# Attention with a routed MoE on one core: the small blocks' first product in two column halves, and a new layout of the PSUM banks in the block loop

## The chip, the cores and the metric

One Trainium2 chip, one of its cores. The metric is the device time of one execution in microseconds (us). Before the change it is 514.08 us, the median of 3 runs (513.99 to 514.44).

## What is computed

Sigmoid attention over 8 batches and 12 heads of 448 tokens with 64 columns, whose result, 3584 tokens of 768 columns, goes through a mixture of experts with a skip:

```python
scores = scale * np.matmul(q, k.transpose(0, 1, 3, 2)) - np.log(S)
attn = 1.0 / (1.0 + np.exp(-scores))
x = np.matmul(attn, v)                  # then 3584 tokens x 768
do_compute = x @ w_skip > 0             # the other tokens are passed on
e_idx = np.argmax(xc @ w_gate, axis=1)  # xc: the tokens to compute; 8 experts
for e in range(8):
    h = np.maximum(xc[mask] @ w1[e], 0.0)         # 768 -> 1024
    y[mask] = gate_w[mask, None] * (h @ w2[e])    # 1024 -> 768
out[do_compute] = xc + y
```

## The kernel before

Up to about 290 us the kernel does the attention and, as each batch is ready, the routing logits. Two blocks of 128 tokens (b0, b1) of the first expert follow with a fixed program, and beside them the lists of tokens for each expert are made. From 313.64 us a loop (L1553 to L1555) runs blocks of tokens; each iteration reads a code word and takes one of four arms:

- FULL and SPLIT (function `block`, L1351): 128 rows. The weights have been split into two parts (wh, wl), the rows too (xh, xl), and each product is the sum of three. SPLIT converts the next expert's weights besides.
- HALF (`half`, L1468): at most 64 rows. The raw f32 weights are used; an f32 matmul leaves two records in the trace. Two matmuls at a time go to two groups of 64 columns of the array.
- FEW (`few`, L1408): at most 32 rows, likewise with raw weights, four matmuls at a time on four groups of 32 columns.

With this input there are fourteen: SPLIT, HALF, FULL, HALF, FULL, FEW, FULL, FEW, FULL, FEW, SPLIT, FEW, FULL, FEW. So seven are large, two HALF, five FEW.

A small block does, in this order on TensorE: the first product (rows times w1) into ph; six transposes of the next block's rows (turn_x, L492, from xn into pxt); the transposes of hs (into pht, a line in each of `few` and `half`: L1442, L1497); the second product (ht times w2) into py. ScalarE (ACT) does the relu from ph to hs (L1433, L1489) and, after the transposes, copies the turned rows to ht (L1444, L1503). Then it turns pxt into the next block's xh, with VectorE (DVE) making xl. SyncE (SP) issues the loads of the next weights: raw1 (`load_w1`, L1234) behind the first product, raw2 (`load_w2`) behind the second. GpSimd (POOL) fetches the rows and the record of coming blocks (`fetch`, from L1286 on) and scatters the results (`put`, `scatter`, L574). In the large blocks, DVE multiplies py by the gate into ys (`weigh_sum`, L1349), in two halves of 384 columns.

The order of the instructions of an arm is as written; semaphore waits between engines are added by the framework, from which instruction touches which tile. PSUM has eight banks of 512 f32 a partition. Here they are given to two two-bank tiles (`new_s`, [P, 2, 512], by turns s0 and s1), three single ones (`new_t`) and one single one (ps_b). In the loop, ph is two single tiles, py is one two-bank tile, pht is another (its second half and the free ph tile serve a small block's two turned parts as `turned = (pht[0], ph[1])`), and pxt is one tile of ps_b and one of new_t.

`addr_align` (L1159), ahead of part of b1's second product, places the code that follows at an offset in a fetch block of TensorE's instructions.

Of the kernel before, what the change touches and what calls it, by code (L numbers as in the profile page):

```python
# [10 lines left out]
F32 = mybir.dt.float32  # L11
# [3 lines left out]
AF = mybir.ActivationFunctionType  # L15
ALU = mybir.AluOpType
# [7 lines left out]
def kernel(  # L24
# [117 lines left out]
    def new_s(name):  # L142

        turn[0] ^= 1
        return ps_s.tile([P, 2, 512], F32, tag=f"s{turn[0]}", name=name)
# [102 lines left out]
    def new_t(name):  # L248

        if ps_t is None:  # L250
            return new_s(name)[:, 0, :]
        return ps_t.tile([P, 512], F32, tag="t", name=name)
# [236 lines left out]
    def turn_x(x, h, px):  # L489
        for j in range(3):  # L490
            i = 3 * h + j
            nc.tensor.transpose(  # L492
                px[:, j * P : (j + 1) * P], x[:, i * P : (i + 1) * P], ident
            )
# [43 lines left out]
    def gemm2(j, hh, hl, py):  # L538
        h, m = divmod(j, 4)
        js = slice(m * P, (m + 1) * P)  # L540
        kinds = ((hh, wh2), (hh, wl2), (hl, wh2))
        terms = [(n, o) for n in range(3) for o in range(2)]
        if j == NK2 - 1:
            terms.sort(key=lambda t: t[::-1])
        for n, o in terms:
            a, w = kinds[n]
            last = nc.tensor.matmul(  # L547
                py[:, o, :H2],
                a[h][:, js],
                w[j][:, o * H2 : (o + 1) * H2],  # L550
                start=(j == 0 and n == 0),
                stop=(j == NK2 - 1 and n == 2),
            )
        return last

    def finish(ys, py, gate, x):
        for o in range(2):
            s = slice(o * H2, (o + 1) * H2)
            nc.vector.scalar_tensor_tensor(
                ys[:, s], py[:, o, :H2], gate, x[:, s], op0=ALU.mult, op1=ALU.add  # L560
            )

    def gather(dst, idx, rows=NT):
# [248 lines left out]
    def new_ph(j):  # L812
        one = new_s(f"b{j}_ph")
        return [one[:, 0, :], ps_b.tile([P, 512], F32, tag="b", name=f"b{j}_ph1")]

    def relu0(h, ph):
        nc.scalar.activation(hs0[h], ph[h], AF.Relu)

# [33 lines left out]
    lg = turn_logits(lb, pl)  # L852
    store_rows(lb, NPAIR - 1, turn_rows(lb, NPAIR - 1))
    ph = new_ph(0)
    py = new_s("b0_py")
    gemm1(0, range(9), xh0, xl0, ph)
    rec, _ = rt = route(lb, lg)
    weigh_route(lb, rt)
# [292 lines left out]
    relu0(1, ph)  # L1151
    nc.vector.tensor_copy(rid[:, 1:2], recs[:, 1, 1:2])
    gather(xn, rid[:, 1:2])
    py = new_s("b1_py")
    for j in range(2):
        gemm2(j, hh0, hl0, py)
    turn0(1)
    nc.tensor.addr_align(bass.FETCH_BLOCK_INSTRUCTIONS, offset=0, max_nops=0)
    for j in range(2, NK2 - 3):  # L1159
        gemm2(j, hh0, hl0, py)  # L1160
    pxt = [ps_b.tile([P, 512], F32, tag="b", name="pxt0"), new_t("pxt1")]
    for h in range(2):
        turn_x(xc, h, pxt[h])
        hi_x(h, pxt[h], xh)
    for h in range(2):
        whole_x(h, [slice(j, j + 1) for j in range(3)])
# [55 lines left out]
    raw1 = [[raw1g[h, i // 3][:, i % 3, :] for h in range(2)] for i in range(NK1)]  # L1222
    raw2 = [raw2g[j // 2][:, j % 2, :] for j in range(NK2)]

    ph = [new_t(f"ph{h}") for h in range(2)]
    py = new_s("py")
    pht2 = new_s("pht")
    pht = [pht2[:, h, :] for h in range(2)]

    def next_expert(word):  # L1230
        return word & (NE - 1), (word & (2 * NE)) >> (2 * NE).bit_length() - 1
# [119 lines left out]
    def block(i, last):  # L1351


        def split1(js, h):
            if last:
                for j in js:
                    hi1(j, h)
                for j in js:
                    lo1(j, h)

        gemm1(0, range(G1), xh, xl, ph, last)
        relu(0, hs, ph)
        split1(range(3), 0)
        gemm1(1, range(9), xh, xl, ph, last)
        turn_h(0, hs, pht[0])
        split_h(0, pht[0], hh, hl)
        take_rec()
        split1(range(3, NK1), 0)
        gemm1(1, range(9, G1), xh, xl, ph, last)
        relu(1, hs, ph)  # L1370
        for h in range(2):
            turn_x(xn, h, pxt[h])
        fetch()
        split1(range(3), 1)
        gemm2(0, hh, hl, py)
        turn_h(1, hs, pht[1])
        split_h(1, pht[1], hh, hl)
        split1(range(3, NK1), 1)
        if last:
            for h in range(2):  # L1380
                whole_x(h, (slice(0, 3),))
            shift(dve)
        else:
            ready_x()
        for j in range(1, NK2):
            gemm2(j, hh, hl, py)
        if last:
            for j in range(2):
                hi2(j)
            for h in range(2):  # L1390
                hi_x(h, pxt[h], xh)
            for j in range(2, NK2):
                hi2(j)
            for j in range(4):
                lo2(j)
            for h in range(2):
                lo_x(h, pxt[h], xh, xl)
        else:
            shift(dve)
        for o in range(2):  # L1400
            weigh_sum(ys[:, o * H2 : (o + 1) * H2], py[:, o, :H2], recs[:, 0, 0:1])
        put(P)
        advance(1 if last else 2)
        if last:
            for j in range(4, NK2):
                lo2(j)

    def few(i, word):  # L1408

        nx = next_expert(word)  # L1410
        for o in range(2):
            nc.vector.tensor_copy(gate2[o * SM : (o + 1) * SM], recs[:SM, 0, 0:1])  # L1412
        take_rec()

        def quarter(dst, g, n, a, w, j, most):
            nc.tensor.matmul(  # L1416
                dst[g * SM : (g + 1) * SM, :n],
                a,
                w,
                start=(j == 0),  # L1420
                stop=(j == most - 1),
                tile_position=(0, g * SM),
            )

        Q1 = FF // 4
        for j in range(NK1):
            for g in range(4):
                s = slice((g % 2) * Q1, (g % 2 + 1) * Q1)
                quarter(ph[0], g, Q1, xf[:, j, :SM], raw1[j][g // 2][:, s], j, NK1)
        turned = (pht[0], ph[1])  # L1430
        parts = [slice(c * P, (c + 1) * P) for c in range(2)]
        for s in parts:
            nc.scalar.activation(hs[:, s], ph[0][:, s], AF.Relu)  # L1433
        for h in range(2):
            for g in range(2):
                load_w1(g, h, nx)
        for h in range(2):
            turn_x(xn, h, pxt[h])
        fetch()
        ht4 = ht[:, : 8 * SM].rearrange("p (c g t) -> p c g t", c=2, g=4)  # L1440
        for s, p in zip(parts, turned):
            nc.tensor.transpose(p[:, :P], hs[:, s], ident)  # L1442
        for s, p in zip(parts, turned):
            nc.scalar.activation(ht[:, s], p[:, :P], AF.Copy)  # L1444
        ready_x()
        shift(dve)

        for n, j in enumerate((0, 2, 1, 3)):
            for g in range(4):
                h, o = g // 2, g % 2  # L1450
                m = j + h * (NK2 // 2)
                quarter(
                    py[:, 0, :],
                    g,
                    H2,
                    ht4[:, j % 2, 2 * h + j // 2, :],
                    raw2[m][:, o * H2 : (o + 1) * H2],
                    n,
                    NK2 // 2,
                )  # L1460
        for g in range(4):
            load_w2(g, nx)
        nc.scalar.activation(yh, py[MD:, 0, :H2], AF.Copy, scale=gate2)
        nc.vector.scalar_tensor_tensor(yt, py[:MD, 0, :H2], gate2, yh, op0=ALU.mult, op1=ALU.add)
        put(SM)
        advance()

    def half(i, word):  # L1468
# [11 lines left out]
                tile_position=(0, g * MD),  # L1480
            )

        for j in range(NK1):
            for h in range(2):
                side(ph[0], h, H1, xf[:, j, :], raw1[j][h], j, NK1)
        turned = (pht[0], ph[1])
        parts = [slice(0, 2 * P), slice(2 * P, 4 * P)]
        for s in (slice(0, P), slice(P, 2 * P), parts[1]):
            nc.scalar.activation(hs[:, s], ph[0][:, s], AF.Relu)  # L1489
        for h in range(2):  # L1490
            for g in range(2):
                load_w1(g, h, nx)
        for h in range(2):
            turn_x(xn, h, pxt[h])
        fetch()
        for c in range(4):
            nc.tensor.transpose(  # L1497
                turned[c // 2][:, (c % 2) * P : (c % 2 + 1) * P],
                hs[:, c * P : (c + 1) * P],
                ident,  # L1500
            )
        for s, p in zip(parts, turned):
            nc.scalar.activation(ht[:, s], p[:, : 2 * P], AF.Copy)  # L1503
        ready_x()
# [3 lines left out]
        for n in range(NK2):  # L1508
            c, h = divmod(n, 2)
            m = h * (NK2 // 2) + c  # L1510
            for o in range(2):
                side(
                    py[:, 0, :],
                    o,
                    H2,
                    ht8[:, c, h, :],
                    raw2[m][:, o * H2 : (o + 1) * H2],
                    n,
                    NK2,
                )  # L1520
        for g in range(4):
            load_w2(g, nx)
        for o in range(2):
            s = slice(o * H2, (o + 1) * H2)
            weigh_sum(ys[:MD, s], py[o * MD : (o + 1) * MD, 0, :H2], recs[:MD, 0, 0:1])
        put(MD)
        advance()

# [55 lines left out]
```

## Time and profile before

| | |
|---|---|
| profiled execution, device time | 514.12 us |
| its span on the core | 512.4 us |
| median of the runs | 514.08 us |
| mean granted TensorE clock | 0.993 |
| TensorE (PE) busy | 499.9 us (98%) |
| DVE / ACT / POOL busy | 294.5 / 271.8 / 258.8 us |
| first of the loop's blocks starts | 313.64 us |
| last matmul of the loop's last block ends | about 503 us |

The timeline view gives, for each run of like instructions on an engine, the start in us from the span's start, the time until the last of them ends, the line, the operation, the output and input tiles, shapes and the count; in brackets the idle time ahead of it and what ended it. Matmuls overlap in the array, so that the time of a run is longer by a part of its last matmul than the distance to the next run.

### The profile page before, as it was taken

What the parts mean: (1) busy time and instruction counts of PE and PEld (TensorE: products, weight loads), DVE (VectorE), ACT (ScalarE), POOL (GpSimd) and SP (SyncE); (2) the same over time, 40 slices, a digit from 0 to 9 for tenths busy, and PEclk for the clock granted to TensorE, in tenths of its full rate; (3) what the DMA queues carried; (4) which work ended last, traced back from release to release, by engine and by line L of the source; (5) the groups of instructions that cost most, each with busy time, mean ns of one, the idle gap of its engine ahead of it and who ended that gap; (6) DMA issues with size and microseconds to landing.
All of it is one profiled execution on the core that took longest, in us unless ns stands there. A gap on an engine that the chain in (4) does not pass through costs nothing. (4 is left out here: it accounts for less than half of the span.)

```text
span 512.4 us, 15271 instructions
## 1 busy us (share of the span) xinstructions
PE 499.9 (98%) x4982; PEld 335.9 (66%) x4983; DVE 294.5 (57%) x745; ACT 271.8 (53%) x480; POOL 258.8 (51%) x405
## 2 busy tenths in 40 slices
PE   8999999999999999999999999999999999999992
PEld 5665555555555555555557988948678787878781
DVE  5565756647868688687785842962132222249432
ACT  5776776767667677677664212933212323259322
POOL 5523455443565786657775341444223434347644
PEclk9999999999999999999999999999999999999997
DMA  7799586677698977897845035979393969697953
GB/s 231 189 235 257 144 205 158 151 172 210 168 240 235 234 198 200 214 261 193 216 99 110 2 95 166 367 226 333 90 373 119 312 246 309 253 315 254 329 214 50
DMA packets 139716, 107.27 MB, mean 209 GB/s; under 512 B 96263, under 2 KB 112265, under 8 KB 139664
## 3 DMA queue, kind: packets, MB, share of 16 engines
q1 hardware_dynamic: 133264, 97.66, 64.5%
q0 software_dynamic: 4736, 8.66, 7.0%
q8 instruction: 33, 0.54, 0.4%
q10 hardware_dynamic: 1664, 0.26, 0.3%
q14 instruction: 19, 0.16, 0.1%
HBM read 98.49 MB, written 17.60 MB: 227 GB/s over the span
## 5 line engine op out<-in xcount | busy, mean ns | idle before, releaser
L256 ACT ACTIVATE at<-s,bias 128x896 f32<-128x896 f32 (+1 forms) x191 | 170.8, 914 | 77.7 <-PE s L236 76.8
L264 PE MATMUL pa<-at,v 64*64 64x448 f32 (+1 forms) x1528 | 161.8, 490 | 0.0
L236 PE MATMUL s<-x 64*64 64x448 f32 (+1 forms) x1504 | 160.6, 494 | 0.3 <-DVE x L216 0.2
L180 POOL COPY kq<-kq 32x896 f32<-32x896 f32 (+1 forms) x96 | 88.0, 917 | 83.7 <-DMA kq<-in_q_dram 41.2
L236 PEld LDWEIGHTS s<-x 64*64 64x64 f32 x1504 | 78.0, 191 | 52.1 <-ACT at L256 20.4
L264 PEld LDWEIGHTS pa<-at,v 64*64 64x64 f32 x1528 | 61.0, 133 | 55.7 <-issue 46.9
L216 DVE STREAM_TRANSPOSE x<-kq 128x448 f32<-128x448 f32 x94 | 82.0, 946 | 4.2 <-POOL kq L180 4.2
L274 DVE TENSOR_TENSOR xt<-xt,pa 128x448 f32<-128x448 f32 x48 | 29.7, 620 | 60.8 <-ACT xt L684 59.5
L486 POOL TENSOR_TENSOR wl<-wr,wh 128x384 fp32r<-128x384 f32 (+1 forms) x28 | 31.3, 1123 | 21.1 <-DVE wh L485 18.9
L413 POOL DMA_INDIRECT lst<-rec,idx x32 | 32.5, 1016 | 13.8 <-DVE nf L923 6.0
L525 ACT ACTIVATE hs<-ph 128x512 f32<-128x512 f32 x14 | 8.4, 598 | 45.9 <-PE ph L516 38.0
L279 DVE STREAM_TRANSPOSE y<-xt 128x448 f32<-128x448 f32 x48 | 31.0, 645 | 1.7
L547 PE MATMUL py<-wh,hh 128*128 128x384 f32 x112 | 31.2, 349 | 0.0
L547 PE MATMUL py<-wl,hh 128*128 128x384 f32 x112 | 29.9, 338 | 0.0
L547 PE MATMUL py<-wh,hl 128*128 128x384 f32 x112 | 29.8, 337 | 0.0
L536 DVE TENSOR_TENSOR hl<-pht,hh 128x512 fp32r<-128x512 f32 x14 | 9.7, 690 | 33.5 <-ACT hh L535 32.2
L516 PE MATMUL ph<-wl,xh 128*128 128x512 f32 x84 | 26.6, 403 | 0.0
L684 ACT ACTIVATE xt<-pa 128x448 f32<-128x448 f32 x48 | 25.7, 536 | 1.2 <-PE pa L264 1.2
L516 PE MATMUL ph<-wh,xh 128*128 128x512 f32 x84 | 25.7, 403 | 0.0
L1349 DVE TENSOR_SCALAR ys<-py,recs 128x384 f32<-128x384 f32 (+1 forms) x18 | 10.4, 612 | 26.0 <-PE py L547 20.8
L502 DVE TENSOR_TENSOR xl<-pxt,xh 128x384 fp32r<-128x384 f32 x30 | 15.3, 552 | 16.5 <-issue 6.5
L516 PE MATMUL ph<-wh,xl 128*128 128x512 f32 x84 | 24.4, 395 | 0.0
(292 smaller groups left out, 683.5 us busy)
## 6 DMA issues: line engine op xcount, KB each, us to landing
raw<-in_moe_w_dram SPq DMA_DIRECT2D x64, 768.0 KB
v<-in_v_dram SPq DMA_DIRECT2D x47, 256.0 KB
out_dram<-y SPq DMA_DIRECT2D x192, 56.0 KB
kq<-in_k_dram SPq DMA_DIRECT2D x23, 448.0 KB
kq<-in_q_dram SPq DMA_DIRECT2D x23, 448.0 KB
wr<-in_moe_w_dram SPq DMA_DIRECT2D x12, 256.0 KB
wr<-in_moe_w_dram SPq DMA_DIRECT2D x16, 192.0 KB
lst<-fill SPq DMA_DIRECT2D x4, 464.0 KB
```

The lines of the kernel that those rows point to most:

```text
L180: nc.gpsimd.tensor_copy(a[to, :, :, :BT], a[at, :, :, BT:])
L216: nc.vector.transpose(xs[:, n].rearrange("p (r j) -> p j r", j=NJ), t.rearrange("p (j d) -> p j d", d=D)[:, :, :BT],)
L236: nc.tensor.matmul(sc[m * D : (m + 1) * D, j, : qs.stop - qs.start], xs[r, 0, first::NR7], xs[r, 1, qs], start=True, stop=True,)
L256: nc.scalar.activation(at[:, :, :n], sc[:, :, :n], AF.Sigmoid, bias=bias, scale=SCALE)
L264: nc.tensor.matmul(pa[j * D : (j + 1) * D, r, qs], vt[r][j][:, c if r == j else (c + 1) % NV, :], at[rs, j, : qs.stop - qs.start], start=( ...
L274: nc.vector.tensor_tensor(x, x, pa[:, 1, :S], op=ALU.add)
L279: nc.vector.transpose(y, xts[b][:, hp, :])
L413: put = nc.gpsimd.indirect_dma_start(out=lst[:, :], out_offset=bass.IndirectOffsetOnAxis(ap=idx[:, c : c + 1], axis=0), in_=rec[:, c, :], ...
L486: nc.gpsimd.tensor_tensor(lo, r, hi, op=ALU.subtract)
L516: nc.tensor.matmul(ph[h], a[:, j * P : (j + 1) * P], w[j][h], start=(n == 0), stop=(n == len(t) - 1),)
L547: last = nc.tensor.matmul(py[:, o, :H2], a[h][:, js], w[j][:, o * H2 : (o + 1) * H2], start=(j == 0 and n == 0), stop=(j == NK2 - 1 and n ...
L684: nc.scalar.activation(xts[b][:, hp, :], pa[:, 0, :S], AF.Copy)
```

## The change

In `few` and `half` the first product is done in two halves of its columns, c = 0 and 1, the first into ph[0], the second into ph[1]. In `few` each half has 24 matmuls of 128 columns in place of 24 of 256 for the whole; in `half`, 12 of 256 columns in place of 12 of 512. The relu of a half stands behind it. The transposes of the first half's hs (one in `few`, two in `half`) stand ahead of the six turn_x, those of the second half behind. The two turned parts go to the two banks of pht, one two-bank tile, in place of one bank of pht and the tile ph[1].

In the loop py becomes two single-bank tiles, ph[0] moves to ps_b, and pxt becomes a two-bank tile. b0 and b1 keep a two-bank tile for py, indexed by a list now. In the fixed part, both turn_x of xc stand ahead of both hi_x. The offset of addr_align goes from 0 to 172.

```diff
-                py[:, o, :H2],
+                py[o][:, :H2],
...
+    def new_banks(name):
+        two = new_s(name)
+        return [two[:, o, :] for o in range(2)]
...
-    nc.tensor.addr_align(bass.FETCH_BLOCK_INSTRUCTIONS, offset=0, max_nops=0)
+    nc.tensor.addr_align(bass.FETCH_BLOCK_INSTRUCTIONS, offset=172, max_nops=0)
...
-    pxt = [ps_b.tile([P, 512], F32, tag="b", name="pxt0"), new_t("pxt1")]
+    pxt = new_banks("pxt")
     for h in range(2):
         turn_x(xc, h, pxt[h])
+    for h in range(2):
         hi_x(h, pxt[h], xh)
...
-    ph = [new_t(f"ph{h}") for h in range(2)]
-    py = new_s("py")
-    pht2 = new_s("pht")
-    pht = [pht2[:, h, :] for h in range(2)]
+    ph = [ps_b.tile([P, 512], F32, tag="b", name="ph0"), new_t("ph1")]
+    py = [new_t(f"py{o}") for o in range(2)]
+    pht = new_banks("pht")
...
# few
-        for j in range(NK1):
-            for g in range(4):
-                s = slice((g % 2) * Q1, (g % 2 + 1) * Q1)
-                quarter(ph[0], g, Q1, xf[:, j, :SM], raw1[j][g // 2][:, s], j, NK1)
-        turned = (pht[0], ph[1])
+        turned = pht
         parts = [slice(c * P, (c + 1) * P) for c in range(2)]
-        for s in parts:
-            nc.scalar.activation(hs[:, s], ph[0][:, s], AF.Relu)
+        for c, s in enumerate(parts):
+            for j in range(NK1):
+                for g in range(4):
+                    at = (g % 2) * Q1 + c * P
+                    quarter(ph[c], g, P, xf[:, j, :SM], raw1[j][g // 2][:, at : at + P], j, NK1)
+            nc.scalar.activation(hs[:, s], ph[c][:, :P], AF.Relu)
+        nc.tensor.transpose(turned[0][:, :P], hs[:, parts[0]], ident)
         for h in range(2):
             for g in range(2):
                 load_w1(g, h, nx)
...
-        for s, p in zip(parts, turned):
-            nc.tensor.transpose(p[:, :P], hs[:, s], ident)
+        nc.tensor.transpose(turned[1][:, :P], hs[:, parts[1]], ident)
         for s, p in zip(parts, turned):
             nc.scalar.activation(ht[:, s], p[:, :P], AF.Copy)
...
# half
-        for j in range(NK1):
-            for h in range(2):
-                side(ph[0], h, H1, xf[:, j, :], raw1[j][h], j, NK1)
-        turned = (pht[0], ph[1])
+        turned = pht
         parts = [slice(0, 2 * P), slice(2 * P, 4 * P)]
-        for s in (slice(0, P), slice(P, 2 * P), parts[1]):
-            nc.scalar.activation(hs[:, s], ph[0][:, s], AF.Relu)
+        for s, one, pieces in zip(parts, ph, ((slice(0, P), slice(P, 2 * P)), (slice(0, 2 * P),))):
+            for j in range(NK1):
+                for h in range(2):
+                    side(one, h, 2 * P, xf[:, j, :], raw1[j][h][:, s], j, NK1)
+            for p in pieces:
+                nc.scalar.activation(hs[:, s][:, p], one[:, p], AF.Relu)
+        for c in range(2):
+            turn_piece(c)
...
         for h in range(2):
             turn_x(xn, h, pxt[h])
         fetch()
...
+        for c in range(2, 4):
+            turn_piece(c)
```

## Rows read from the trace of the kernel before

**Rows 1.** The page: span, busy time of each engine with its share of the span and its instructions, and TensorE's granted clock in 40 slices of the span, in tenths.

```profile
span 512.4 us, 15271 instructions
...
PE 499.9 (98%) x4982; PEld 335.9 (66%) x4983; DVE 294.5 (57%) x745; ACT 271.8 (53%) x480; POOL 258.8 (51%) x405
...
PEclk9999999999999999999999999999999999999997
```

**Rows 2.** Timeline of TensorE, the first HALF block and the first run of the FULL block behind it.

```profile
332.25 5.37 PE L1474 MATMUL ph<-raw,xf 128*64 128x512 f32 x24
337.55 0.87 PE L492 MATMUL pxt<-ident,xn 128*128 128x128 f32 x6
338.26 0.38 PE L1497 MATMUL pht<-ident,hs 128*128 128x128 f32 x2
338.64 0.41 PE L1497 MATMUL ph<-ident,hs 128*128 128x128 f32 x2
339.16 5.38 PE L1474 MATMUL py<-raw,ht 128*64 128x384 f32 x32
344.48 1.67 PE L516 MATMUL ph<-wh,xh 128*128 128x512 f32 x6
```

**Rows 3.** The same timeline, the first FEW block, from the last matmul of the FULL block ahead of it.

```profile
393.54 0.34 PE L547 MATMUL py<-wh,hl 128*128 128x384 f32 x1
393.81 2.80 PE L1416 MATMUL ph<-raw,xf 128*32 128x256 f32 x48
396.54 0.87 PE L492 MATMUL pxt<-ident,xn 128*128 128x128 f32 x6
397.25 0.30 PE L1442 MATMUL pht<-ident,hs 128*128 128x128 f32 x1
397.47 0.30 PE L1442 MATMUL ph<-ident,hs 128*128 128x128 f32 x1
397.97 2.90 PE L1416 MATMUL py<-raw,ht 128*32 128x384 f32 x32 [0.19 <-DVE gate L1412]
```

**Rows 4.** Timeline of the other engines in that FEW block: DVE, SP's queue, ACT.

```profile
393.98 1.14 DVE L1349 TENSOR_SCALAR ys<-py,recs 128x384 f32<-128x384 f32 x2 [4.16 <-PE py L547]
...
395.55 3.85 SPq L1234 DMA_DIRECT2D raw<-in_moe_w_dram  x4
...
396.83 0.45 ACT L1433 ACTIVATE hs<-ph 128x128 f32<-128x128 f32 x2 [8.11 <-PE ph L1416]
...
397.59 0.28 ACT L1444 ACTIVATE ht<-pht 128x128 f32<-128x128 f32 x1 [0.31 <-PE pht L1442]
397.60 0.32 DVE L1412 COPY gate<-recs 32x1 f32<-32x1 f32 x2 [1.89 <-ACT hs L1433]
```

**Rows 5.** Timelines of TensorE and of DVE, the FEW block that begins at 470.42.

```profile
473.23 0.88 PE L492 MATMUL pxt<-ident,xn 128*128 128x128 f32 x6
474.63 2.90 PE L1416 MATMUL py<-raw,ht 128*32 128x384 f32 x32 [0.19 <-ACT ht L1444]
...
477.04 0.31 DVE L1412 COPY gate<-recs 32x1 f32<-32x1 f32 x2
```

**Rows 6.** Timeline of ACT in the first HALF block.

```profile
337.78 0.72 ACT L1489 ACTIVATE hs<-ph 128x128 f32<-128x128 f32 x3 [2.16 <-PE ph L1474]
...
338.68 0.38 ACT L1503 ACTIVATE ht<-pht 128x256 f32<-128x256 f32 x1 [0.18 <-PE pht L1497]
```

**Rows 7.** Timeline of TensorE in the attention part, a run of the routing logits (48 matmuls, four at a time on groups of 32 columns); the line view of that line (count: fastest, median and slowest in ns, from and to in us); and of L1416 the semaphore steps of TensorE's sequencer in five FEW blocks, likewise.

```profile
42.83 1.36 PE L296 MATMUL pl<-xt,wcat 128*32 128x112 f32 x48
...
L296 PE MATMUL pl<-xt,wcat x336: 258/259/284, 42.8 to 245.6; 128*32 128x112 f32 x168
...
L1416 PEldq EVENT_SEMAPHORE  x80: 51/51/214, 392.4 to 500.5; - x80
```

**Rows 8.** Timelines of TensorE and ACT at two places of the fixed part: transposes of rows into b_px, one two-bank tile, and into pxt, two single tiles, and ACT's reads of them, half by half.

```profile
273.96 0.87 PE L492 MATMUL b_px<-ident,x 128*128 128x128 f32 x6
...
274.93 0.87 ACT L498 ACTIVATE b<-b_px 128x384 fp32r<-128x384 f32 x2 [0.28 <-PE b_px L492]
...
309.82 0.84 PE L492 MATMUL pxt<-ident,xc 128*128 128x128 f32 x6
...
310.36 0.87 ACT L498 ACTIVATE xh<-pxt 128x384 fp32r<-128x384 f32 x2 [2.88 <-PE pxt L492]
```

**Rows 9.** Windows: a stretch of the FEW block that begins at 419.36. Columns: the stretch and its length; busy us and instructions (x) of PE, PEld, DVE, ACT and POOL; granted clock; mean busy share of the DMA engines; GB/s.

```profile
419.40:422.00 2.60, 2.60 (x49) 1.42 (x48) 1.67 (x7) 0.00 (x0) 0.68 (x2) 1.00 0.00 0
```

**Rows 10.** Timelines of TensorE and POOL in the last FEW block.

```profile
498.16 1.62 POOL L574 DMA_INDIRECT out_dram<-ys,rp  x1 [0.58 <-issue]
...
498.73 0.87 PE L492 MATMUL pxt<-ident,xn 128*128 128x128 f32 x6
...
499.75 0.26 POOL L1286 TENSOR_TENSOR xn<-xn,zf 128x1 f32<-128x1 f32 x1
...
506.02 1.49 POOL L574 DMA_INDIRECT out_dram<-yt,rh  x1 [0.53 <-issue]
```

**Rows 11.** DMA queues of the whole span (the page: packets, MB, share of 16 engines), and all that moved packets from 330 to 505 us.

```profile
q8 instruction: 33, 0.54, 0.4%
...
q1 hardware_dynamic: 16253, 38.08, 59.9%
q0 software_dynamic: 3023, 6.35, 15.7%
```

More of the change, by code (lines that the diff above doesn't have):

```diff
@@ L559, in finish @@
             nc.vector.scalar_tensor_tensor(
-                ys[:, s], py[:, o, :H2], gate, x[:, s], op0=ALU.mult, op1=ALU.add
+                ys[:, s], py[o][:, :H2], gate, x[:, s], op0=ALU.mult, op1=ALU.add
             )
@@ L854 @@
     ph = new_ph(0)
-    py = new_s("b0_py")
+    py = new_banks("b0_py")
     gemm1(0, range(9), xh0, xl0, ph)
@@ L1153 @@
     gather(xn, rid[:, 1:2])
-    py = new_s("b1_py")
+    py = new_banks("b1_py")
     for j in range(2):
@@ L1400, in block @@
         for o in range(2):
-            weigh_sum(ys[:, o * H2 : (o + 1) * H2], py[:, o, :H2], recs[:, 0, 0:1])
+            weigh_sum(ys[:, o * H2 : (o + 1) * H2], py[o][:, :H2], recs[:, 0, 0:1])
         put(P)
@@ L1452, in few @@
                 quarter(
-                    py[:, 0, :],
+                    py[0],
                     g,
@@ L1462, in few @@
             load_w2(g, nx)
-        nc.scalar.activation(yh, py[MD:, 0, :H2], AF.Copy, scale=gate2)
-        nc.vector.scalar_tensor_tensor(yt, py[:MD, 0, :H2], gate2, yh, op0=ALU.mult, op1=ALU.add)
+        nc.scalar.activation(yh, py[0][MD:, :H2], AF.Copy, scale=gate2)
+        nc.vector.scalar_tensor_tensor(yt, py[0][:MD, :H2], gate2, yh, op0=ALU.mult, op1=ALU.add)
         put(SM)
@@ L1481, in side, with turn_piece @@
             )
-        for j in range(NK1):
-            for h in range(2):
-                side(ph[0], h, H1, xf[:, j, :], raw1[j][h], j, NK1)
-        turned = (pht[0], ph[1])
-        parts = [slice(0, 2 * P), slice(2 * P, 4 * P)]
-        for s in (slice(0, P), slice(P, 2 * P), parts[1]):
-            nc.scalar.activation(hs[:, s], ph[0][:, s], AF.Relu)
+        def turn_piece(c):
+            nc.tensor.transpose(
+                turned[c // 2][:, (c % 2) * P : (c % 2 + 1) * P],
+                hs[:, c * P : (c + 1) * P],
+                ident,
+            )
+        turned = pht
+        parts = [slice(0, 2 * P), slice(2 * P, 4 * P)]
+        for s, one, pieces in zip(parts, ph, ((slice(0, P), slice(P, 2 * P)), (slice(0, 2 * P),))):
[6 more added lines that the diff above has]
+            turn_piece(c)
         for h in range(2):
@@ L1495, in half @@
         fetch()
[L1496 to L1501, printed above, removed]
+        for c in range(2, 4):
+            turn_piece(c)
         for s, p in zip(parts, turned):
@@ L1512, in half @@
                 side(
-                    py[:, 0, :],
+                    py[0],
                     o,
@@ L1524, in half @@
             s = slice(o * H2, (o + 1) * H2)
-            weigh_sum(ys[:MD, s], py[o * MD : (o + 1) * MD, 0, :H2], recs[:MD, 0, 0:1])
+            weigh_sum(ys[:MD, s], py[0][o * MD : (o + 1) * MD, :H2], recs[:MD, 0, 0:1])
         put(MD)
```

## The prediction

> **What bounds the kernel now.** I read the busy table and the clock row first [rows 1]: TensorE is busy 499.9 of 512.4 us, at the 2.4 GHz level to the end. So only what lengthens or shortens TensorE's own sequence, or the few stretches in which it stands still, can move the time. I then read TensorE's timeline over the block loop. Between blocks there is nothing to win: a HALF's second product starts at 339.16, lasts 5.38 and overlaps the next block's first matmul at 344.48 [rows 2]. TensorE stands still inside the small blocks alone, between the first and the second product, and that is where the change works. The loop runs seven large blocks (block), two HALF (half) and five FEW (few).
>
> FEW [rows 3]: first product from 393.81, six row transposes (pxt) at 396.54, one transpose of hs at 397.25, the other at 397.47, second product (py) at 397.97. So pxt to py is 1.43 us. Of this, the pxt slots take 0.71 (396.54 to 397.25); then one hs transpose of 0.30, ACT's copy into ht from 397.59 (0.28) [rows 4], and 0.10 from its end at 397.87 to py. In that block the view names DVE's gate copy as releaser of py; in the block of 474.63 it names ACT's ht copy, and there the gate copy runs at 477.04, after py has begun [rows 5]. So ACT's first ht copy is what py waits for; DVE is not.
>
> HALF [rows 2, 6]: pxt 337.55, two hs transposes at 338.26 (0.38 for both), two at 338.64, the first ht copy at 338.68 (0.38), py at 339.16: 1.61 us.
>
> **The change, part by part.** *First product in halves.* The columns stay the same, the instructions double. FEW: 24 matmuls become 48, in the trace 48 records become 96, in fours on four column groups. Now twelve fours of 256 columns take 396.54 - 393.81 = 2.73, or 0.228 each [rows 3]. The nearest row of fours with few columns is the routing product: 48 records with 112 columns in 1.36, the last one 0.26 long, so (1.36 - 0.26) / 11 = 0.100 a four, or 0.114 scaled to 128 columns [rows 7]. 24 x 0.114 = 2.74 against 2.73: nothing. The other bound is the sequencer: if the new half needs up to four more semaphore steps of 51 ns [rows 7] that don't hide, +0.20. I take +0.05, near the row that has the work itself. HALF: 24 records of 512 columns take 5.30 [rows 2], 48 of 256 columns the same by columns; I take +0.02, bounds 0 and +0.10. A gain I exclude: the columns to be streamed are unchanged.
>
> *What the halving hides.* The first half's relu now runs below the second half's matmuls. But relu does not hold up py now: it runs from 396.83 for 0.45, below pxt [rows 4], and the first hs transpose starts 0.71 after pxt, when the slots of pxt are through. What it allows is that the first hs transposes go ahead of pxt.
>
> *The turned halves in one two-bank tile.* This decides the sign. Whether a reader of one bank waits for writes to the other bank of the same tile is shown twice. In the prologue, six transposes go into one pair from 273.96 for 0.87 and ACT's first read, of the first three, starts at 274.93, after all six. With two separate tiles they start at 309.82 and ACT's read at 310.36, 0.54 later, while the last still run [rows 8]. In the loop py is a pair now: the last matmul (second half) starts at 393.54 and lasts 0.34, and DVE's ys of the first half starts only at 393.98 [rows 3, 4]. So the first ht copy, which now waits for the first transpose alone, will wait for the last one. FEW after, from the end of the first product: transpose 0 at 0 (a slot of 0.71 / 6, or 0.11), pxt 0.11 to 0.82, transpose 1 at 0.82, its end (0.30) 1.12, copy 1.16 to 1.44, py at 1.54 against 1.43: **+0.11**. The second half's relu, about half of the 0.45 beginning 0.29 after the product's end, is done by 0.73 with room for its latency, before 0.82. HALF after: transposes 0 and 1 at 0 to 0.22, pxt 0.22 to 0.93, transposes 2 and 3 from 0.93, end (0.38) 1.31, copy 1.35 to 1.73, py at 1.83 against 1.61: **+0.22**. The third relu piece, now begun some 0.23 after the product as the first is today (337.78) [rows 6], is done long before 0.93.
>
> *Output halves in tiles of their own.* In the seven large blocks DVE's ys of the first half starts some 0.5 us sooner. Nobody on TensorE's path waits for it: the next product's py is over 3 us away [rows 3], and ys, two of 0.57 in 1.14 [rows 4], end by 395.12. Cost and gain 0. What would be late if this cover were gone: the scatter of the rows, on POOL, off the path until the last block.
>
> *pxt as a pair.* ACT's first xh copy then waits for six transposes instead of three: three slots, 0.33. In the loop that copy comes behind the ht copies on ACT, after all six; in the prologue it is 310.36 to 310.69 [rows 8], three microseconds ahead of the first loop block. 0.
>
> *Weight loads.* raw1's next load is issued on SP from 395.55 on [rows 4], as the first product frees its groups. In halves, a group is free only when the second half has read it: later by up to a quarter of 2.73 in FEW (0.7) and of 5.30 in HALF (1.3). Queued behind it on SP are only raw2's loads. From 419.40 to 422.00, while TensorE runs a FEW's first product, no transfer is in flight (share 0.00) [rows 9]: 2.6 us of cover. Cost 0; without that cover, up to 1.3 us a small block.
>
> *Loop code and its alignment.* The loop grows by 24 + 12 matmuls, each two records with two weight loads: 144 instructions, and its head moves within the fetch block. Instruction packets take 0.4% of 16 engines' span for 33 blocks, 0.4% x 16 x 512.4 / 33 = 1.0 us a block, and from 330 to 505 only q1 and q0 move packets [rows 11]: once through, the loop's code is fetched no more. I take 0.
>
> *Sum.* The last FEW ends the program through POOL: its L1286 at 499.75 follows pxt (498.73) and the scatter from 498.16 for 1.62 (both end within 0.2), and the last scatter is at 506.02 [rows 10]. pxt is later by 0.11 + 0.05 there, py likewise, so 0.16 counts in that block too. FEW 5 x (0.11 + 0.05) = 0.80, HALF 2 x (0.22 + 0.02) = 0.48: **+1.28 us**. On the profiled execution's 514.12 that is 515.40; it lies 0.04 above the median of 514.08, so 515.4 for the median as well. Bounds: 5 x 0.11 + 2 x 0.22 = +0.99, and 5 x 0.31 + 2 x 0.32 = +2.19; with the runs' own spread (513.99 to 514.44), **514.8 to 516.6**. A measurement of this kernel can tell about 0.2%, 1.03 us, from no change.
>
> **Rivals.** *A, the pair's banks are waited for apart (faster).* Then the first ht copy starts once transpose 0 is through: FEW 0.30, copy 0.34 to 0.62, but TensorE has pxt and transpose 1 until 0.93, and py starts at about 1.03: 0.40 less, net of 0.06 for the stream 0.34 in four blocks; the last still loses 0.16 through pxt and POOL. HALF: py at about 1.25 against 1.61, 0.34 net twice. -1.36 + 0.16 - 0.68 = -1.9: **512.2**. For it: the two halves do lie in different banks, and where the tiles are separate the reader starts early [rows 8]. Against it: both readings of pairs, in the prologue and in py [rows 3, 4, 8]. 15%.
>
> The Trainium skill's page PSUM — Partial Sum Buffer, section "PSUM bank collisions raise a hardware error", asks for a guard "by bank × quadrant"; by it halves in two banks need no wait on each other, and A would come out. The rows of the prologue's pair disagree for this program: its waits are wider than the rule.
>
> *B, the longer loop is fetched again (slower).* If 144 more instructions no longer stay with the engine, each of 14 iterations pays at least one block of 1.0 us on a TensorE that never waits: +14, **529**; if only some iterations do, 517 to 520. It decides from the point where the loop outgrows what stays. For it: nothing in the trace shows how much more code would stay. Against it: no packet in 175 us of 14 blocks [rows 11]. 9%.
>
> The skill's page Runtime: NRT & Kernel Launch, section "Instruction fetch mechanics", says that a taken branch out of a two-block window forces a fetch. By that the loop would pay now already; the window without instruction packets does not show it.
>
> *C, the change does nothing on the path (same).* If py is released in effect by something else of equal lateness, as the view says with DVE's gate in four of five FEW, the shift of 0.11 is swallowed: **514.1 to 514.6**. Against it: the block in which the gate copy runs after py has begun [rows 5]. 6%.
>
> **How the numbers follow.** Forecast 70%: its centre is +1.28, and with an uncertainty of half a microsecond some 45 of these 70 lie above +1.03, 25 below. A 15% is faster (512.2 is 1.9 under), B 9% slower, C 6% same. Slower 0.54, same 0.31, faster 0.15. The range must leave out no more than 2 in 10: the forecast and C give 76, so it reaches down over A to 512.0, and leaves B out above 516.6.
>
> **What would show it.** In FEW, one hs transpose stands ahead of pxt, py starts 1.54 after it, and ACT's first ht copy starts only when the second hs transpose has ended; in HALF py starts 1.83 after the first hs transpose. 96 records of the FEW product take 2.7 to 2.9. ys of the first half starts while the last py matmuls still run. No instruction packets after 330. Wrong if the ht copy starts before the second hs transposes (A), if TensorE idles at a block's head with instruction packets (B), if py is unmoved with ht done earlier (C), or if a first product waits on raw.

## The result and the profile after

The changed kernel takes 517.85 us (517.03 to 518.69) against 514.22: 1.0065 times the kernel before, 95% interval 1.0053 to 1.0077, so slower by 3.6 us. In a second set of runs on another chip it is 517.93 against 514.71, 1.0064 (1.0051 to 1.0076). The sign was forecast; the size, 1.3 us, was not, and the time lies above the range. The profiled execution took 518.17 us.

The page of the changed kernel answers to [rows 1]: TensorE is busy for 0.3 us more, the span is 4.1 longer. So the loss is nearly all time in which TensorE stands still.

```profile
span 516.5 us, 15803 instructions
...
PE 500.2 (97%) x5270; PEld 351.3 (68%) x5271; DVE 295.8 (57%) x745; ACT 271.7 (53%) x480; POOL 257.1 (50%) x405
```

The ledger below takes each block from the start of its first product to the start of the next block's, on TensorE's timeline of both profiled executions.

| stretch | before | after | difference |
|---|---|---|---|
| span's start to b1's last matmul | 313.47 | 314.08 | +0.61 |
| b1's last matmul to the loop's first | 0.17 | 1.49 | +1.31 |
| seven large blocks, together | 129.89 | 129.74 | -0.15 |
| two HALF | 12.22, 12.23 | 12.71, 12.67 | +0.93 |
| FEW behind FULL, the first three | 6.99, 6.99, 7.01 | 7.22, 7.22, 7.22 | +0.67 |
| FEW behind SPLIT | 7.04 | 8.36 | +1.32 |
| the last FEW's start to the span's end | 16.40 | 15.76 | -0.64 |

The first line is not the change's: the transposes into b_px, ahead of the work of every changed line, already start at 274.62 in place of 273.96 [rows 8], and in the runs below b1's last matmul starts between 313.25 and 316.57 without order. I therefore compare stretches.

**The entry of the loop.** TensorE's timeline after, b1's last matmul and the loop's first; where before there were 0.17 between them (313.47 and 313.64), there are 1.49 now. "issue" means that the engine waited for nothing that the profile shows.

```profile
314.08 0.34 PE L547 MATMUL b_py<-wh,b 128*128 128x384 f32 x1
315.56 0.47 PE L516 MATMUL ph<-wh,xh 128*128 128x512 f32 x1 [1.15 <-issue]
```

The view of the branch's line (fastest, median and slowest in ns, from and to in us) shows what the sequencer did: of the eight branches at that line, the slowest took 2003 ns; it is the first, from 313.40 to 315.40. Before (L1548) the first was the slowest too, with 255.

```profile
L1558 PEldq COMPARE_BRANCH  x8: 73/198/2003, 313.4 to 470.6; - x8
```

```profile
L1548 PEldq COMPARE_BRANCH  x8: 73/196/255, 312.7 to 467.2; - x8
```

From 330 to 505 us no instruction packets move, as before [rows 11].

```profile
q1 hardware_dynamic: 16361, 38.40, 60.2%
q0 software_dynamic: 2817, 5.90, 14.6%
```

**FEW**, TensorE and ACT of the changed kernel; it answers to [rows 3, 4].

```profile
396.52 2.85 PE L1420 MATMUL ph<-raw,xf 128*32 128x128 f32 x96
...
399.30 0.33 PE L1438 MATMUL pht<-ident,hs 128*128 128x128 f32 x1
...
399.46 0.82 PE L492 MATMUL pxt<-ident,xn 128*128 128x128 f32 x6
...
400.12 0.27 PE L1446 MATMUL pht<-ident,hs 128*128 128x128 f32 x1
...
400.43 0.45 ACT L1448 ACTIVATE ht<-pht 128x128 f32<-128x128 f32 x2 [0.66 <-PE pht L1446]
...
400.91 2.90 PE L1420 MATMUL py<-raw,ht 128*32 128x384 f32 x32 [0.52 <-issue]
```

The first product takes 2.78, 0.05 more, as forecast. The first hs transpose ends at 399.63, yet ACT copies at 400.43, after the second one (400.39). py comes 1.61 after the first transpose; 1.54 was forecast. It starts 0.20 after the end of the first copy (400.71), where before there were 0.10 (397.87 to 397.97). In HALF, answering to [rows 2, 6], it is 341.46 - 339.47 = 1.99 in place of 1.83:

```profile
339.47 0.44 PE L1488 MATMUL pht<-ident,hs 128*128 128x128 f32 x2
...
339.75 0.82 PE L492 MATMUL pxt<-ident,xn 128*128 128x128 f32 x6
...
340.40 0.38 PE L1488 MATMUL pht<-ident,hs 128*128 128x128 f32 x2
...
340.87 0.66 ACT L1513 ACTIVATE ht<-pht 128x256 f32<-128x256 f32 x2 [0.84 <-DVE wl L1265]
...
341.46 5.38 PE L1478 MATMUL py<-raw,ht 128*64 128x384 f32 x32 [0.67 <-issue]
```

Here the view puts the copy's wait down to DVE's wl, which ends at about the same time as the last transpose (340.86 and 340.78). e5, below, tells them apart: there the same wl runs until 341.66, and the copy starts at 340.76.

**FEW behind SPLIT** is the surprise. Its first product stops at 40 of 96 records and takes 477.72 - 473.80 = 3.92 us. ACT's timeline has SPLIT's last six weight conversions from 471.36 for 4.55, to 475.91; the product goes on at 476.05.

```profile
471.36 4.55 ACT L1262 ACTIVATE wh<-raw 128x768 fp32r<-128x768 f32 x6
...
473.80 1.94 PE L1420 MATMUL ph<-raw,xf 128*32 128x128 f32 x40
...
476.05 1.74 PE L1420 MATMUL ph<-raw,xf 128*32 128x128 f32 x56 [0.31 <-ACT wh L1262]
...
477.72 0.33 PE L1438 MATMUL pht<-ident,hs 128*128 128x128 f32 x1
```

Before, the same six conversions ended at 472.52, 2.10 after the block's start at 470.42, and the product's last weight group (40 of 48 records, 10 of 12 fours at 0.228) was due at 470.42 + 2.28 = 472.70. The wait was there, with 0.2 us of cover:

```profile
467.98 4.54 ACT L1258 ACTIVATE wh<-raw 128x768 fp32r<-128x768 f32 x6
```

The product reads raw and xf, and these conversions write neither: in the changed trace xf was written by 469.27, over 4 us ahead of the block. So TensorE waits for ACT to get to the end of its queue, and not for data of these conversions. Which tile made the framework put the wait there is not shown.

```profile
468.73 0.54 ACT L1120 ACTIVATE xf<-pxt 128x192 f32<-128x192 f32 x2
```

**The end.** DVE's ys in the last FEW starts before that block's first product now (500.33, the product 500.69), 0.5 earlier in the block than before, since the first half no longer waits for the second. POOL's scatter follows it: 502.33, 1.64 after the block's start, where before it was 498.16 - 496.00 = 2.16 [rows 10]; the last scatter comes 510.19 - 500.69 = 9.50 after it in place of 10.02.

```profile
500.33 1.14 DVE L1353 TENSOR_SCALAR ys<-py,recs 128x384 f32<-128x384 f32 x2 [3.26 <-PE py L547]
...
502.33 1.62 POOL L574 DMA_INDIRECT out_dram<-ys,rp  x1 [0.58 <-issue]
...
510.19 1.49 POOL L574 DMA_INDIRECT out_dram<-yt,rh  x1 [0.55 <-issue]
```

### The profile page after: what moved, and what is told of

It is laid out like the page before. It is cut to its first block, busy times and chain, and to the rows that moved or that the text cites. A ratio compares the mean times of both kernels' runs of the same rounds, so it can differ in the third digit from the quotient of the medians.

```text
span 516.5 us, 15803 instructions
## 1 busy us (share of the span) xinstructions
PE 500.2 (97%) x5270; PEld 351.3 (68%) x5271; DVE 295.8 (57%) x745; ACT 271.7 (53%) x480; POOL 257.1 (50%) x405
## 4 chain that ended last, share of the span: by engine, by line
PE 93%; DVE 2%; issue 1%; DMA 1%; SPq 1%; ACT 0%; POOLq 0%; ACTq 0%; POOL 0%; DVEq 0%
PE s L236 25%; PE pa L264 25%; PE ph L516 12%; PE py L547 11%; PE py L1420 3%; PE ph L1420 3%; PE b_py L547 2%; PE b_ph L516 2%; PE py L1478 2%; PE ph L1478 2%; PE pxt L492 2%; PE pl L296 2%; PE pht L530 1%; DMA v<-in_v_dram 1%; PE b_pht L826 0%
## 5 line engine op out<-in xcount | busy, mean ns | idle before, releaser
L264 PE MATMUL pa<-at,v 64*64 64x448 f32 (+1 forms) x1528 | 167.8, 490 | 0.6 <-DMA v<-in_v_dram 0.6
L236 PE MATMUL s<-x 64*64 64x448 f32 (+1 forms) x1504 | 165.7, 494 | 0.0
L236 PEld LDWEIGHTS s<-x 64*64 64x64 f32 x1504 | 82.7, 191 | 48.2 <-issue 19.3
L264 PEld LDWEIGHTS pa<-at,v 64*64 64x64 f32 x1528 | 65.5, 133 | 54.1 <-issue 45.2
```

The costliest lines, as they stand in the source:

```text
L236: nc.tensor.matmul(sc[m * D : (m + 1) * D, j, : qs.stop - qs.start], xs[r, 0, first::NR7], xs[r, 1, qs], start=True, stop=True,)
L264: nc.tensor.matmul(pa[j * D : (j + 1) * D, r, qs], vt[r][j][:, c if r == j else (c + 1) % NV, :], at[rs, j, : qs.stop - qs.start], start=( ...
```

## Experiments

Theory now: four causes, each with its place. P, the code's placement stalls the first branch; T, the pair makes the first ht copy wait for the last transpose; H, the halves bring the last weight groups' first use forward into a wait that was covered; and a smaller one in the bank layout. Runs of one set share a chip and the runs of the kernel before; e11 alone, told with the third set, ran on the chip of the second.

### First set: placement, and the late groups

The kernel before took 519.97 us on this chip. Edits: e1, `offset=172` to `offset=0`; e2, to `offset=216`; e3, the kernel before with `offset=172`.

> The changed kernel with addr_align's offset back at 0 (as before), all else as changed. In the changed trace the branch into the first block's arm took 2.00 us on TensorE's sequencer (0.26 before), with an instruction fetch from 312.80, and the first matmul of the loop came 1.31 us later after b1's last one than before. Theory P (placement: the loop's head lies so close behind a fetch block's start that the code two blocks on is not there yet at the first branch): with offset 0 the branch is short again and the gap from b1's last matmul to the loop's first is 0.17 us as before; total 517.85 - 1.3 = 516.5. Rival S (the gap is a wait for xl or xh, made later by the pxt pair): the gap stays at 1.49 us, 517.8. Rival L (without the alignment the longer loop spans one fetch block more and is fetched again in each iteration): instruction packets in the loop, 14 x 1 us, above 528.

> The changed kernel with offset 216 in place of 172: the loop's head moves 44 instructions further into its fetch block, so that the block is entered some 22 matmuls (about 3.8 us) ahead of the head, and the loop lies in as many fetch blocks as with 172. P: no gap at the loop's entry, 516.5, and no instruction packets in the loop. S: gap of 1.49 us as with 172, 517.8.

> The kernel before with offset 172 and nothing else. P: the entry gap appears in the kernel before too, first loop matmul 1.3 us later, 514.2 + 1.3 = 515.5; blocks unchanged (HALF 12.22, FEW 6.99 to 7.10 us). S: no gap, 514.2.

Measured: e1 528.14 (1.0161, 1.0142 to 1.0180), e2 524.00 (1.0079, 1.0062 to 1.0095), e3 520.66 (1.0018, 1.0004 to 1.0031). The gap from b1's last matmul to the loop's first is 2.66, 0.17 and 1.53 us. So P holds and S falls: the offset alone puts the gap into the kernel before, which has neither halves nor pair. The totals cannot carry this. The changed kernel did not run on this chip, and against the kernel before e1 is 8.2 us slower and e2 4.0, where 2.3 were forecast for both; e3 is 0.7 slower (interval 0.2 to 1.6), where 1.3 were forecast. The branch's line in e1, e2 and e3:

```profile
L1558 PEldq COMPARE_BRANCH  x8: 73/204/4067, 313.8 to 479.0; - x8
```

```profile
L1558 PEldq COMPARE_BRANCH  x8: 73/192/250, 315.9 to 475.1; - x8
```

```profile
L1548 PEldq COMPARE_BRANCH  x8: 73/191/2082, 315.1 to 472.7; - x8
```

In e1 the slowest, 4067, is the second pass, into the first HALF; the first branch took 3187:

```profile
L1558 PEldq COMPARE_BRANCH  x1: 3187/3187/3187, 313.8 to 313.8; - x1
```

The instruction packets of the traces bear P out. With offset 172 the changed kernel's packet of 16 KB runs from 312.80 to 313.96, so that it begins only 0.60 ahead of the slow branch; in e1 it begins behind it (314.52, the branch 313.83). In the kernel before it had run from 306.14 on and in e2 from 311.84, over 4 us ahead of the branch. In all six runs with a gap (the changed kernel, e0, e1, e3, e4, e5) the branch ends 1.41 to 1.44 us after such a packet has ended.

For e1 I had forecast no gap, and its 2.66 shows that offset 0 is good for the short loop only; I take it that the arms of the longer one lie elsewhere in the fetch blocks. Its first SPLIT took 21.37 and its first HALF 14.40 besides (18.50 and 12.71 with 172), yet from 340 to 515 us it moves q1 and q0 packets alone, so L falls: the code is fetched once, and only that first pass is paid.

e4 takes the last two weight groups late:

```diff
-        for c, s in enumerate(parts):
-            for j in range(NK1):
+        for js in (range(4), range(4, NK1)):
+            for c, s in enumerate(parts):
+                for j in js:
...
+                if js.stop == NK1:
+                    nc.scalar.activation(hs[:, s], ph[c][:, :P], AF.Relu)
```

> The changed kernel, but the FEW block's first product takes weight groups j = 0 to 3 for both column halves first, then j = 4 and 5 for the first half (with its relu) and for the second. In the changed trace the FEW block behind the second SPLIT took 8.36 us against 7.22 in the others: TensorE got to group j = 3, 4, 5 half as late as before and waited there for ACT's conversions of SPLIT, the last of which ended at 475.91, 2.1 us after the block's start. Theory H (halving brings the last groups' first use forward, from 2.28 to 1.14 us after the start): with the last groups late, that block takes 7.3 to 7.6, the other FEW 7.22; total 517.85 - 0.9 = 516.9. Rival W (that block was held by its weight loads or by a chance of this run): it stays above 8.2, or the stall wanders to another block, 517.8.

Measured 526.27 (1.0128, 1.0106 to 1.0150). The block behind SPLIT took 7.87 in place of 8.36, but each FEW behind FULL 8.57. On this chip FEW blocks stall for half a microsecond that the others don't show (last section), so that this run decides nothing on H but that block's 0.49.

### Second set: the pair

e0 is the changed kernel again. e5 gives the second turned part the bank of ph[0], whose relu is long done; in `few` and `half`:

```diff
-        turned = pht
+        turned = (pht[0], ph[0])
```

e6 has the changed kernel's tiles with the arms of before and offset 0; e7 is e5 with offset 216.

> The changed kernel unchanged, as the yardstick for the others of this set on the same chip (two chips have shown 514 and 520 us for the kernel before). If the four causes read from the trace are the whole of it (entry of the loop +1.3, HALF 2 x 0.45, FEW 5 x 0.23, FEW behind SPLIT +1.1, last blocks -0.5), it is 3 to 4.5 us over the kernel before. Rival: part of the loss was the one execution's own, and it is under 2 us here.

> The changed kernel, the second turned half in ph[0]'s bank, a tile of its own, in place of the pair's second bank; nothing else. Theory T (ACT's first ht copy waits for the pair's last write): the copy starts once the first half's transposes are through, py follows the last transpose closely: HALF from 12.7 to about 12.0 us, FEW from 7.22 to about 6.8, in sum 2 x 0.65 + 5 x 0.4 = 3.3 us less than the changed kernel. Rival Q (the extra 0.1 us and more ahead of py is TensorE's own sequencer, which steps through its semaphore waits in order): the blocks shorten by under 0.2 us each, under 1.2 us in all.

> The changed kernel's bank tiles (py in two single tiles, ph[0] in ps_b, pxt as a pair), but the small blocks' first product, transposes and turned tiles as before and offset 0. If the layout is free, as predicted, blocks are those of before (HALF 12.22, FEW 7.0) and only the end is shorter, since ys of the first half starts 0.5 us sooner and POOL's chain in the last FEW with it: 0.5 us under the kernel before. Rival X (pxt as a pair delays xh where it matters): 0.3 us or more over the kernel before.

> The changed kernel with the turned halves apart as in e5 and offset 216 as in e2. If T and P hold and add: the changed kernel less 3.3 for the blocks and less what the offset gives (1.3 at the loop's entry, less what the first pass through the other arms costs, 0.6 to 1.1 in the run with 216): about the kernel before or 1 us under it. Rival: the gains don't add, 2 us or more above the kernel before.

Measured against 514.71: e0 517.93 (+3.2), e5 513.67 (0.9986, 0.9976 to 0.9996), e6 514.75 (1.0000, 0.9991 to 1.0009), e7 513.54 (0.9975, 0.9964 to 0.9985). e5 is 4.3 us under e0 for one line in each arm. HALF goes from 12.68 and 12.63 to 11.98 and 11.88, FEW from 7.24 to 6.57, the one behind SPLIT from 8.35 to 7.66: 1.45 + 3 x 0.67 + 0.69 = 4.15. T holds, Q falls. TensorE and ACT in e5's FEW: the ht copy starts 0.36 after the first hs transpose, below pxt, and py 0.20 after the second.

```profile
398.64 0.33 PE L1438 MATMUL pht<-ident,hs 128*128 128x128 f32 x1
...
398.80 0.82 PE L492 MATMUL pxt<-ident,xn 128*128 128x128 f32 x6
...
399.00 0.28 ACT L1448 ACTIVATE ht<-pht 128x128 f32<-128x128 f32 x1
...
399.46 0.27 PE L1446 MATMUL ph<-ident,hs 128*128 128x128 f32 x1
...
399.66 2.79 PE L1420 MATMUL py<-raw,ht 128*32 128x384 f32 x32
```

e6 is not free in its parts: HALF 12.33, FEW 7.10, each 0.11 longer than before, and 9.45 from the last FEW's start to the last scatter, 0.57 shorter; 7 x 0.11 against 0.57 leaves nothing to measure, where 0.5 us less than the kernel before was forecast. In its first FEW the idle time ahead of py is 0.30 where it was 0.19 [rows 3]:

```profile
397.92 0.30 PE L1446 MATMUL ph<-ident,hs 128*128 128x128 f32 x1
398.52 2.90 PE L1420 MATMUL py<-raw,ht 128*32 128x384 f32 x32 [0.30 <-ACT ht L1448]
```

The view of the second product's line shows the semaphore steps of TensorE's sequencer just ahead of py, first before, then in e6:

```profile
L1416 PEldq EVENT_SEMAPHORE  x2: 51/105/159, 397.6 to 397.8; - x2
```

```profile
L1420 PEldq EVENT_SEMAPHORE  x2: 51/158/264, 398.1 to 398.4; - x2
```

There are two in both, but in another order. Before, the long one, which ends 0.04 after the first ht copy (397.91, the copy 397.87), is the last. In e6 the long one ends 0.04 after the copy too (398.36, the copy 398.32), and the one of 51 ns comes behind it, from 398.42; py follows at 398.52. The changed kernel has the same order.

In e7 the loop's entry is clean (0.17), but TensorE starves in the first SPLIT, which takes 19.40 in place of 18.50:

```profile
315.96 0.39 PE L516 MATMUL ph<-wh,xl 128*128 128x512 f32 x1
316.91 0.50 PE L516 MATMUL ph<-wh,xh 128*128 128x512 f32 x1 [0.56 <-issue]
```

### Third set: offset 209, late groups, banks

e8 is e7 with `offset=209`, e9 is e8 with e4's loops, e10 is e9 with the banks of before. e11, run beside the kernel before on a chip of the second set, is e9 with the first hs transpose between the row transposes of either half:

```diff
-        nc.tensor.transpose(turned[0][:, :P], hs[:, parts[0]], ident)
...
-        for h in range(2):
-            turn_x(xn, h, pxt[h])
+        turn_x(xn, 0, pxt[0])
+        nc.tensor.transpose(turned[0][:, :P], hs[:, parts[0]], ident)
+        turn_x(xn, 1, pxt[1])
```

> As e7 (turned halves apart), but offset 209 in place of 216. With 216 the branch into the first block was short (its code had been fetched from 309.96, before the head), but the SPLIT block behind it took 19.40 us against 18.6, with TensorE starved for 0.56 us from 316.0, just behind a fetch from 314.48. Theory P, made exact: the first arm's code starts 14 instructions ahead of the next fetch block with 216; with 209 it is 21, seven more instructions or some 0.8 us, while the head's own block is still entered 0.6 us sooner than its code is needed. Then both first-pass stalls vanish: gap from b1's last matmul to the loop's first 0.2 to 0.4, SPLIT 18.5 to 18.7, 0.8 us under e7, 1.9 under the kernel before. Rival: a first-pass stall of 0.5 us or more shows at either place and the total is e7's.

> As e8, and FEW's first product takes weight groups 4 and 5 last for both halves (as in e4). Theory H: the FEW block behind SPLIT, 7.66 us with the halves apart against 6.57 in the other four, falls to 6.6 to 6.8 (the first half's relu starts 0.46 us ahead of the product's end and is still in time), the others stay at 6.57: 1.0 us under e8. Rival W (not the order of the groups): it stays at 7.66; or the later relu delays the first transpose, and every FEW grows by 0.1 or more.

> As e9, but with the banks of the kernel before (py one two-bank tile, ph in two new_t tiles, pxt in two single tiles). The layout alone made each small block 0.11 us longer, by one more semaphore step of TensorE ahead of py, and the last block's end 0.5 us shorter. If both come from the layout, here the seven small blocks are 0.1 us shorter each than in e9 and the stretch from the last FEW's start to the last scatter is 10.0 less 0.5 us for the shorter block, in place of 9.5: within 0.5 us of e9. Rival: the small blocks keep their length (the step belongs to the halves), 0.5 us slower than e9.

> As e9 (late groups, halves apart, offset 209), but FEW's first hs transpose stands between the three row transposes of either half in place of ahead of all six. In e9 the four FEW behind a FULL block grew from 6.57 to 6.93 us, while the one behind SPLIT fell from 7.66 to 7.18. If the 0.37 is TensorE waiting at the first transpose for the relu that now starts later, three row transposes (0.33) cover it: FEW 6.6 to 6.7, behind SPLIT 6.8 to 7.0; total 1.2 us under e9 and 0.3 to 0.6 under e8, some 1.5 us under the kernel before. Rival: the 0.37 comes from the other order of the weight groups in the product itself, and FEW stays at 6.9.

Measured against 514.55: e8 513.49 (0.9981, 0.9972 to 0.9990), e9 514.44 (0.9996, 0.9987 to 1.0005), e10 514.91 (1.0006, 0.9997 to 1.0015); e11 514.34 against 514.61 (0.9996, 0.9987 to 1.0005).

| block | before | changed | e5 | e7 | e8 | e9 | e11 |
|---|---|---|---|---|---|---|---|
| entry gap | 0.17 | 1.49 | 1.43 | 0.17 | 0.17 | 0.17 | 0.17 |
| first SPLIT | 18.61 | 18.50 | 18.50 | 19.40 | 18.61 | 18.68 | 18.59 |
| HALF behind it | 12.22 | 12.71 | 11.98 | 11.98 | 13.30 | 12.04 | 13.31 |
| second HALF | 12.23 | 12.67 | 11.88 | 11.88 | 11.88 | 11.88 | 11.88 |
| second FEW | 6.99 | 7.22 | 6.57 | 6.55 | 6.55 | 6.94 | 6.82 |
| FEW behind SPLIT | 7.04 | 8.36 | 7.66 | 7.66 | 7.66 | 7.18 | 7.09 |

With 209 both first-pass stalls are gone, as P said. But against the kernel before the total stays at e7's, 1.1 us under it in place of the 1.9 forecast, because HALF behind SPLIT is now 1.3 longer: it had come sooner, and it waits as FEW does behind the other SPLIT. This is H at a second place.

```profile
332.07 1.95 PE L1478 MATMUL ph<-raw,xf 128*64 128x256 f32 x16
334.91 3.94 PE L1478 MATMUL ph<-raw,xf 128*64 128x256 f32 x31 [0.89 <-ACT wh L1262]
```

ACT's timeline of e8 shows that the last two conversions began late themselves, after 1.23 us of idling, and the first of them ended (333.92 + half of 1.58) as TensorE went on:

```profile
329.61 3.07 ACT L1262 ACTIVATE wh<-raw 128x768 fp32r<-128x768 f32 x4
333.92 1.58 ACT L1262 ACTIVATE wh<-raw 128x768 fp32r<-128x768 f32 x2 [1.23 <-issue]
```

In the kernel before they began as late, at 334.04, and HALF, whose fifth of six groups is due only at 332.25 + 4/6 x 5.30 = 335.8, did not notice. In e9 they ran without the idling, and its HALF took 12.04; in e10 it took 13.26. The weight packets (q1) of the traces point to what they wait for: the last one ends at 333.42 in e8, 332.16 in e9, 334.16 in e10 and 334.18 in e11, and these conversions begin 0.50 to 0.59 us later in each. Nothing that e9 changes touches them, so its 12.04 belongs to that execution, the fastest of its eleven (513.18), and not to its code.

e9 confirms H and its price: behind SPLIT 7.66 falls to 7.18 (6.6 to 6.8 was forecast), but the other FEW grow by 0.37, since the first half now ends late and its transpose waits for the relu: it starts 3.00 after the product's start in place of 2.78. In e11 three row transposes cover a third of the 0.37, so that where the rest lies is not shown. Neither is worth it: e9's four FEW lose more than the one gains. e10's second HALF and its FEW are as long as e9's (11.88 and 6.93), so that the 0.11 of the layout, seen in e6, is not on the path once the halves are turned apart; the rival came true. This fits e5's trace, where the same two steps start at 399.25 and 399.43, ahead of the second hs transpose. e10's profiled execution (516.72, the slowest of its eleven) also holds a stretch of 0.97 in the second SPLIT that no other run has, and is not used further.

## Why the prediction was wrong

Two terms failed that the sum put at nothing: the loop's code, which cost 1.31 us on the loop's first pass, and the time at which the last weight groups are first used, booked under "Weight loads", which cost 1.09 in one block.

- **Its two-bank step was right, and a little small.** That the first ht copy waits for the pair's last write is shown by e5. It costs FEW 0.67 and HALF 0.70 and 0.74 against tiles apart. Against before, the blocks lost 0.23 and 0.46 where 0.16 and 0.24 were forecast. Of the missing 0.07 and 0.22, 0.10 and 0.11 are the layout's (e6), which I had put at nothing, by looking only at who reads py and pxt: a semaphore step of TensorE (51 ns [rows 7]) that stands behind the wait for the copy now, and ahead of it before. FEW's copy came 0.03 sooner than forecast; HALF's last 0.1 lies in its first product (5.41 and 5.34 for 5.30) and its transposes.
- **"Loop code and its alignment: 0" failed.** That no instruction packets move after the first pass was read rightly and held in every run. But the first pass itself, the one branch at 313, was left out: +1.31, and 1.36 in the kernel before when the offset alone is changed (e3). The prediction said that the loop's head moves within its fetch block, and gave that no price. Rival B named a fetch that TensorE waits for, but had another reason for it, the loop's length, and another count: it comes once, not fourteen times. The Trainium skill's page Runtime: NRT & Kernel Launch, section "Instruction fetch mechanics", has a taken branch out of the current window wait for a fetch. The first branch agrees (2.00 us against 0.26); the later iterations, which move no instruction packet, do not.
- **"Weight loads: 0" asked for the wrong cover.** I checked that the next loads would land in time, from when a group is *freed*. The change moves as well when each group is first *used*: the last one from 10/12 to 5/12 of the product. Behind SPLIT that uncovered ACT's conversions: +1.09 beyond the other FEW's +0.23, and in e8 1.3 in HALF. One of its own signs of being wrong, a first product that waits, came close: it waits for ACT, and not for raw.
- **The end.** I let pxt set POOL's start in the last FEW, as the two were 0.2 apart, and booked +0.16. It was the scatter before it, and so ys: -0.5, in e6, which has no halves, too. Here the single py tiles do earn something.
- **The sum.** Forecast +1.28. Measured by stretches: 1.31 + 0.93 + 0.67 + 1.32 - 0.64 - 0.15 = +3.44, beside +3.6 and +3.2 of the medians. Of this, 1.31 + 1.09 = 2.4 are the two terms at 0. The sum's lower bound has a slip of its own: 513.99 + 0.99 is 515.0, not 514.8.

The versions that beat both kernels are e5, e7 and e8, the change with its turned halves apart: 513.5 to 513.7 us, 1.0 to 1.2 us under the kernel before. The three differ in the offset alone, and their totals show no gain from it: what 216 and 209 save at the loop's entry, the first SPLIT or the HALF behind it takes back.

## What to carry to other kernels

When a loop over weight groups is split so that it runs twice over them, each group's first use comes at half its old time: look for every wait of the old loop that had been covered, and at the blocks whose predecessor still works on the same engine's queue. In this program a pair of banks that two steps share was one thing to wait for, and a bank whose reader is done was a better second target. And the loop's code had a price on its first pass, which changed with the offset of its head: compare the first iteration apart from the others.

## What was not expected of the hardware

On the chip of the first set, FEW blocks stall at a place where the profile shows no wait. In e2 TensorE's product stops at 85 of 96 records, with POOL's scatter under way since 426.86:

```profile
425.23 2.61 PE L1420 MATMUL ph<-raw,xf 128*32 128x128 f32 x85
...
426.86 1.63 POOL L574 DMA_INDIRECT out_dram<-ys,rp  x1 [0.58 <-issue]
...
428.15 0.64 PE L1420 MATMUL ph<-raw,xf 128*32 128x128 f32 x11 [0.31 <-issue]
```

In e3, with the code of before, FEW behind FULL takes 7.62 in place of 6.99, and ACT's relu begins late. On the other chips no such stall shows. It comes some 0.7 us after the scatter begins, in e1, e2 and e4 alike (405.06 after 404.30, 427.57 after 426.86, 400.64 after 399.95); what causes it stays open.
